# VectorE builds the table of distances before the slopes, in a kernel of banded attention and a two-layer MLP

## Chip, cores and metric

One NeuronCore of a Trainium2 chip. The metric is the device time of one launch in microseconds (us), as the median of several runs. The engines that matter are TensorE (PE in the profile, its weight loads PEld), VectorE (DVE), ScalarE (ACT), GpSimd (POOL) and SyncE (SP). Each has its own in-order queue of instructions; they meet at semaphores. DMAs are issued from the queues of SP, ACT and POOL.

## The reference

Four batches of eight heads, 768 positions, head size 64. A key is kept when it is one of the first 8 positions or lies up to 95 positions behind the query; the score gets a penalty, slope of the head times distance. The attention output goes through two matrix products with `h - tanh(h)` between them.

```python
rel = pos[:, None] - pos[None, :]
is_global = pos[None, :] < 8
is_local = (rel >= 0) & (rel < 96)
keep = is_global | is_local
dist = np.where(is_global & ~is_local, 96.0, np.abs(rel))
slopes = 2.0 ** (-8.0 * (np.arange(H) + 1) / H)
scores = q @ k.T / 8 - slopes[:, None, None] * dist
scores = np.where(keep, scores, -1e9)
a = softmax(scores)
x = (a @ v) as 3072 rows of 512
h = x @ w_in                    # 512 -> 2048
out = (h - tanh(h)) @ w_out     # 2048 -> 512
```

## The kernel before

The 3072 rows are 24 units of 128 query rows (six per batch), the first units of the four batches coming first. For each unit the kernel loads q, k and v, transposes q and k (`T`, copied out of PSUM by `Te`), multiplies them (`S`), takes the exponential on ScalarE (`E`), multiplies by a mask on VectorE (`M`), multiplies by v (`AV`), divides (`R`), transposes (`X`, `Xe`), and runs the MLP in groups of one, two or four units (`m1`, `th`, `g`, `m2`, `ev`, `st`). Since exp(s + b) = exp(s) exp(b), the penalty and the band are one multiplicative mask `mk` that is made once at the start.

That start is what the change touches:

- `rel` (POOL, L237) writes a tile of row minus column, for the unit's own block and the block behind it.
- `slopes` (DVE, L267) is eight instructions, one for each head: a 128x128 diagonal matrix times that head's slope, all from `rel`. The slots of the heads are interleaved: even heads fill slots 0 to 3, odd heads 4 to 7.
- `dist` (DVE, L242, L243, L244) is three instructions, each needing the one before: the distance inside the band, a huge number outside.
- `turn`, `first`, `ident` and `ones.1` follow on VectorE: a permutation matrix for the transposes, the variant of `dist` for a batch's first unit (L247, L248, L251), an identity matrix, and columns of ones in the tiles of v.
- `bm.1` and `bm.0` (PE, L277) multiply `dist` (loaded as weights) by `slopes` (streamed), two matmuls each, one for slots 0 to 3 and one for slots 4 to 7. `em.1` and `em.0` (ACT, L282) take the exponential and leave the mask.
- `zero:7` and its like (PE, L543) are matmuls of a tile of zeros, put there to keep TensorE running; five of them stand ahead of `bm.1`.
- In the same microseconds the first loads go out: `lk.1`, `lk.0` from SP and `lq.1`, `lq.0` from ACT, in float32 (tiles `f`, L296), which `ck`/`cq` then cast (L233 on DVE, L231 on ACT); and from POOL `lk.2`, `lq.2`, `lq.3`, `lk.3` (tiles `kq`, L296), the v tiles (`vb`, L299) and pieces of the MLP's weights (L302), all cast in flight. `T.1`, `T.0` (PE, L319) are the transposes of units 1 and 0, `S.1`, `S.0` (L354) their scores, `AV.1` (L380) the first product with v.

The order on every engine is written out by hand: one string of words, `ORDER`, is walked from left to right, and each word emits its instructions into the queue of its engine. A framework inserts the semaphore waits that the data needs. Buffers are assigned by a second string, so an engine's queue holds its instructions in the order of the words.

Of the kernel before, what the change touches and what calls it, by code (L numbers as in the profile page):

```python
# [14 lines left out]


ORDER = """
lq.1 lk.1 zero rel ones.0 zero:7 slopes lk.2 lq.0 lk.0 zero:7 zero:7 table lq.2 dist zero:7 zero:7 lq.3 turn bm.1
first lk.3 ident bm.0 ones.1 em.1 lv.1 cq.1/d zero:7 ck.1/a lv.0 zero:7 em.0 T.1 in.0 cq.0/a zero:7 ck.0/d lv.2 zero:7
Te.1.0/d Te.1.1/a zero:3 T.0 lv.3 S.1 Te.0.1/d Te.0.0/a zero:6 zero:6 E.1.0 in.1 S.0 T.2 in.3 E.0.0 M.1.0 T.3 in.2  # L20
Te.2.0/d zero:1 Te.2.1/a AV.1 M.0.0 Te.3.0/a lq.4 S.2 Te.3.1/a R.1 AV.0 lk.4 E.2.0 S.3 R.0 E.3.0 in.4 M.2.0 X.0 zero:3
# [569 lines left out]
```

## Time and profile before

| | |
|---|---|
| median of 3 runs | 212.19 us (211.27, 212.39, 212.19) |
| the profiled execution | 212.06 us, of which its span is 210.2 us |
| outside the span | 1.86 us |
| PE busy | 202.4 us (96%) |
| DVE, ACT, POOL busy | 130.0, 121.7, 79.2 us |
| instructions | 4631 |

The span runs from the first to the last instruction that the profiler recorded; times in the timeline are counted from its start. A timeline row gives the start, the time that the merged instructions took together, the engine, the line, the tiles written and read, how many instructions were merged, and in brackets how long the engine had been idle and who released it. Matmul rows of PE overlap, so the distance between two starts says more than the length of one.

### The profile page before, as it was taken

Reading aid. Unit: us, or ns where it says so; the run is one execution under the profiler, and the core shown is the slowest. Engines: PE = TensorE matmul, PEld = TensorE weight load, DVE = VectorE, ACT = ScalarE, POOL = GpSimd, SP = SyncE. Lnnn points to the kernel's source line nnn. Section 1 sums busy time; section 2 is a strip of 40 time slices with the busy share of each in tenths; the row PEclk is TensorE's granted clock in tenths of the full one; section 3 lists DMA queues with packets and bytes.
Section 4 is the critical chain, followed back from the end, with each engine's and each line's share of the span. In section 5 each row is a group of like instructions: output and inputs, shape, how many; then the busy total and the mean of one; then the engine's idle time right before and its main releaser. Section 6 shows DMA issues by size and latency. Waiting matters only on the chain.

```text
span 210.2 us, 4631 instructions
## 1 busy us (share of the span) xinstructions
PE 202.4 (96%) x1851; PEld 122.3 (58%) x1876; DVE 130.0 (62%) x266; ACT 121.7 (58%) x182; POOL 79.2 (38%) x105
## 2 busy tenths in 40 slices
PE   8779999999999999999999999999999999999994
PEld 2459896566867756887655455545544444444443
DVE  6397786353999963878785489757966661711000
ACT  4797783636887464766845687477457552511251
POOL 8976466503995039807509710002000001000350
PEclk9999999999999999999999999999999999999999
DMA  5999999999999989998999999301610001000255
GB/s 162 195 184 199 190 175 203 180 160 181 141 154 187 188 146 186 143 150 148 174 176 160 142 229 171 59 3 48 176 30 0 0 0 50 3 0 0 101 217 182
DMA packets 101348, 27.29 MB, mean 130 GB/s; under 512 B 91856, under 2 KB 99792, under 8 KB 101328
## 3 DMA queue, kind: packets, MB, share of 16 engines
q0 software_dynamic: 73152, 18.88, 86.2%
q1 hardware_dynamic: 27632, 7.61, 21.5%
q10 hardware_dynamic: 544, 0.52, 0.8%
q8 instruction: 14, 0.23, 0.4%
q14 instruction: 6, 0.05, 0.1%
HBM read 27.26 MB, written 6.29 MB: 160 GB/s over the span
## 4 chain that ended last, share of the span: by engine, by line
PE 92%; DMA 3%; DVE 2%; issue 1%; ACT 1%; SPq 0%
PE ps L422 40%; PE ps L447 39%; PE ps L354 5%; PE ps L380 5%; DMA f<-in_k_dram 3%; PE ps L400 1%; DVE pr L365 1%; DVE x L389 1%; ACT pr L361 0%; PE ps L314 0%; SPq L296 0%; PE ps L319 0%; DVE qk L233 0%; ACT qk L231 0%; PE ps L323 0%
## 5 line engine op out<-in xcount | busy, mean ns | idle before, releaser
L422 PE MATMUL ps<-xT,w_in_bf 128*128 128x256 bf16 (+2 forms) x634 | 89.6, 293 | 0.3
L447 PE MATMUL ps<-w_out_bf,g 128*128 128x512 bf16 (+2 forms) x382 | 88.1, 370 | 1.1 <-issue 0.2
L438 DVE TENSOR_TENSOR g<-ps,th 128x512 bf16<-128x512 f32 (+1 forms) x98 | 65.5, 676 | 31.8 <-ACT th L432 30.8
L432 ACT ACTIVATE th<-ps 128x512 f32<-128x512 f32 (+1 forms) x98 | 57.3, 590 | 45.5 <-PE ps L422 40.5
L422 PEld LDWEIGHTS <-w_in_bf 128*128 128x128 bf16 x640 | 56.2, 98 | 27.2
L447 PEld LDWEIGHTS <-g 128*128 128x128 bf16 x400 | 37.1, 98 | 38.7
L456 POOL DMA_DIRECT2D out_dram<-ot x22 | 12.4, 570 | 105.5 <-ACT ot L231 94.9
L361 ACT ACTIVATE pr<-ps 128x1024 bf16<-128x1024 f32 x44 | 42.9, 1027 | 11.4 <-PE ps L354 10.9
L365 DVE TENSOR_TENSOR pr<-pr,mk 128x1024 bf16<-128x1024 bf16 x44 | 29.7, 687 | 11.4 <-ACT pr L361 11.2
L231 ACT COPY ot<-ps 128x512 f32<-128x512 f32 (+2 forms) x20 | 11.3, 564 | 21.0 <-PE ps L447 15.8
L299 POOL DMA_DIRECT2D vb<-in_v_dram x24 | 21.7, 919 | 3.0 <-DMA w_in_bf<-in_moe_w_in_dram 1.7
L299 POOL DMA_DIRECT2D kq<-in_q_dram x19 | 17.3, 916 | 10.0 <-DMA qk<-kq 7.7
L299 POOL DMA_DIRECT2D kq<-in_k_dram x19 | 17.3, 919 | 2.4 <-DMA w_out_bf<-in_moe_w_out_dram 1.6
L389 DVE TENSOR_TENSOR x<-ps,rden 128x512 bf16<-128x512 f32 x24 | 16.6, 691 | 0.8
L380 PEld LDWEIGHTS <-pr 128*128 128x128 bf16 x352 | 13.6, 97 | 4.0 <-DVE pr L365 0.8
L380 PE MATMUL ps<-vb,pr 128*128 128x65 bf16 x352 | 14.6, 193 | 0.1
L354 PEld LDWEIGHTS <-qk 64*128 64x128 bf16 x352 | 9.9, 94 | 6.2 <-issue 4.0
L354 PE MATMUL ps<-qk 64*128 64x128 bf16 x192 | 9.4, 217 | 0.2 <-ACT qk L231 0.2
L354 PE MATMUL ps<-qk,qk 64*128 64x128 bf16 x160 | 7.8, 217 | 0.0
L388 DVE RECIPROCAL rden<-ps 128x8 f32<-128x8 f32 x24 | 4.8, 199 | 4.6 <-PE ps L380 4.4
L233 DVE COPY qk<-qk 128x32 bf16<-128x32 bf16 x16 | 3.3, 221 | 6.5 <-PE ps L354 6.5
L543 PE MATMUL ps<-zero 128*128 128x512 bf16 x14 | 5.3, 483 | 1.0 <-DVE zero L464 1.0
(43 smaller groups left out, 60.3 us busy)
## 6 DMA issues: line engine op xcount, KB each, us to landing
out_dram<-ot POOLq DMA_DIRECT2D x22, 256.0 KB, 2.9
vb<-in_v_dram POOLq DMA_DIRECT2D x24, 128.0 KB, 6.0
kq<-in_k_dram POOLq DMA_DIRECT2D x22, 128.0 KB, 6.2
kq<-in_q_dram POOLq DMA_DIRECT2D x22, 128.0 KB, 6.2
w_out_bf<-in_moe_w_out_dram POOLq DMA_DIRECT2D x4, 512.0 KB, 11.2
w_in_bf<-in_moe_w_in_dram POOLq DMA_DIRECT2D x4, 256.0 KB, 7.6
w_in_bf<-in_moe_w_in_dram POOLq DMA_DIRECT2D x2, 512.0 KB, 10.7
f<-in_q_dram ACTq DMA_DIRECT2D x2, 256.0 KB, 3.9
```

The lines of the kernel that those rows point to most:

```text
L231: nc.scalar.copy(out=out, in_=in_)
L299: eng(e).dma_start(out=dst, in_=rows_of(src, u).rearrange("h p d -> p h d"))
L354: nc.tensor.matmul(bank(("s", u, o), hh)[:, p * P : (p + 1) * P], buf(("qk", back[u] if o else u))[r, 1, p, :], buf(("qk", u))[r, 0, p, :] ...
L361: nc.scalar.activation(d, banks(("s", u, o), 0, 1), AF.Exp, bias=0.0, scale=scale)
L365: nc.vector.tensor_tensor(out=t, in0=t, in1=mk[:, mask_of(u, o)], op=ALU.mult)
L380: nc.tensor.matmul(t[:, h // (H // 2), h % (H // 2), :], buf(("p", u, o))[:, slot(h), :], buf(("v", back[u] if o else u))[:, h, 0 : Dh + 1 ...
L389: nc.vector.tensor_tensor(out=buf(("x", u)).rearrange("q (a h) d -> q a h d", a=2), in0=t[:, :, :, 0:Dh], in1=rden.to_broadcast([P, 2, H / ...
L422: nc.tensor.matmul(t[:, (f - f0) * n : (f - f0 + 1) * n], w_in_bf[j][:, c, fo : fo + P], x[:, c, 0:n], start=(c == 0), stop=(c == CD - 1),)
L432: nc.scalar.activation(h_view(buf(("th", g, f0)), g, m), h_view(bank(("h", g, f0)), g, m), AF.Tanh, bias=0.0, scale=1.0)
L438: nc.vector.tensor_tensor(out=buf(("g", g))[:, f0 : f0 + m, 0:n], in0=h_view(bank(("h", g, f0)), g, m), in1=h_view(buf(("th", g, f0)), g, ...
L447: nc.tensor.matmul(bank(part)[:, 0 : c1 - c0], buf(("g", g))[:, f, t * P : (t + 1) * P], w_out_bf[f // FJ][:, f % FJ, c0:c1], start=(f == ...
L456: eng(e).dma_start(out=out[turn_of[u] * P : (turn_of[u] + 1) * P, c0:c1], in_=buf(("ot", u))[:, c0:c1])
```

## The change

Two words of `ORDER` trade places: `dist` comes where `slopes` stood, and `slopes` where `dist` stood. Between them stand only words of other engines (loads, zero matmuls, and the word `table`, which emits nothing).

```diff
-lq.1 lk.1 zero rel ones.0 zero:7 slopes lk.2 lq.0 lk.0 zero:7 zero:7 table lq.2 dist zero:7 zero:7 lq.3 turn bm.1
+lq.1 lk.1 zero rel ones.0 zero:7 dist lk.2 lq.0 lk.0 zero:7 zero:7 table lq.2 slopes zero:7 zero:7 lq.3 turn bm.1
```

In the built program the instructions of PE, ACT, POOL and SP keep their order. On VectorE the three instructions of `dist` now stand ahead of the eight of `slopes`; `turn` still follows both. The weight load of `bm.1` waits for `dist` as before; before, that wait covered `slopes` too, since they came earlier on the same engine, and now the two matmuls of `bm.1` each have a wait of their own for `slopes`.

## The prediction

> **What bounds the kernel now.** I read the page first: the span, the busy line, the chain that ended last.
>
> ```profile
> span 210.2 us, 4631 instructions
> ...
> PE 92%; DMA 3%; DVE 2%; issue 1%; ACT 1%; SPq 0%
> ```
>
> 92% of the chain is matmuls; the DMA share is a single load. The chain in order of time (start, length, what) says where it lies, and the table of stretches (PE, PEld, DVE, ACT, POOL busy, granted clock, DMA share, GB/s) how the rest runs.
>
> ```profile
> 0.74 0.74 SPq L296
> 1.54 6.23 DMA f<-in_k_dram
> 8.28 0.63 PE ps L319 x8
> ...
> 0.00:8.28 8.28, 5.90 (x23) 2.00 (x23) 3.87 (x32) 4.73 (x6) 7.46 (x14) 1.00 0.82 182
> 8.28:16.00 7.72, 6.49 (x120) 4.52 (x122) 6.50 (x13) 6.83 (x11) 6.51 (x9) 1.00 1.88 178
> 16.00:210.00 194.00, 190.02 (x1713) 115.75 (x1734) 119.66 (x223) 110.13 (x166) 65.22 (x83) 1.00 1.07 126
> ```
>
> So there are two regimes. From 16 us on PE is busy for 190.02 of 194.00 us, and nothing there is touched by the change except by starting earlier or later. Up to 8.28 us the end is set by one transfer: the float32 load of k for unit 0, issued from SP at 1.54, landing at 1.54 + 6.23 = 7.77 us, after which PE's transposes `T.0` start at 8.28. A microsecond won or lost at 8.28 is passed on nearly whole. The mask work that the change reorders lies in that first regime, beside the load. Its timeline:
>
> ```profile
> 0.99 2.31 PE L543 MATMUL ps<-zero 128*128 128x512 bf16 x5 [0.99 <-DVE zero L464]
> 1.21 0.90 DVE L267 TENSOR_SCALAR slopes<-rel 128x128 bf16<-128x128 bf16 x8 [0.23 <-POOL rel L237]
> 1.37 1.03 POOL L296 DMA_DIRECT2D kq<-in_k_dram  x1 [0.19 <-issue]
> ...
> 2.04 0.22 DVE L242 TENSOR_SCALAR far<-rel 128x256 bf16<-128x256 bf16 x1
> ...
> 2.29 0.43 DVE L243 SCALAR_TENSOR_TENSOR far<-rel,far 128x256 bf16<-128x256 bf16 x1
> 2.40 1.45 POOL L296 DMA_DIRECT2D kq<-in_q_dram  x2
> 2.75 0.29 DVE L244 TENSOR_TENSOR dist<-far,rel 128x256 bf16<-128x256 bf16 x1
> 2.96 0.22 DVE L259 TENSOR_SCALAR turn<-rel 128x128 bf16<-128x128 bf16 x1
> 3.09 0.16 PEld L277 LDWEIGHTS <-dist 128*128 128x128 bf16 x2 [0.69 <-DVE dist L244]
> ...
> 3.40 0.43 DVE L254 TENSOR_SCALAR ident<-rel 128x128 bf16<-128x128 bf16 x1
> ...
> 4.20 1.02 ACT L282 ACTIVATE mk<-ps 128x1024 bf16<-128x1024 f32 x1 [0.77 <-PE ps L277]
> ...
> 4.55 1.77 POOL L299 DMA_DIRECT2D vb<-in_v_dram  x2
> ...
> 7.04 0.60 ACT L231 CAST qk<-ps 128x512 bf16<-128x512 f32 x1
> ...
> 7.79 0.43 DVE L233 CAST kq<-f 128x512 bf16<-128x512 f32 x1 [3.01 <-DMA f<-in_k_dram]
> 8.13 1.28 DVE L233 CAST qk<-ps 128x512 bf16<-128x512 f32 x2
> ...
> 8.28 0.62 PE L319 MATMUL ps<-turn,kq 128*128 128x128 bf16 x8 [1.20 <-DVE kq L233]
> 8.87 0.40 PE L354 MATMUL ps<-qk 64*128 64x128 bf16 x8
> ...
> 11.31 0.41 PE L380 MATMUL ps<-vb,pr 128*128 128x65 bf16 x8
> ```
>
> The weight load of `dist` at 3.09 stands 0.69 us idle and names `dist` as its releaser. That looks like a wait worth removing. The next view, single matmuls cut out by narrow windows, says that it isn't.
>
> ```profile
> 2.67 0.63 PE L543 MATMUL ps<-zero 128*128 128x512 bf16 x1
> 3.10 0.63 PE L277 MATMUL ps<-slopes,dist 128*128 128x512 bf16 x1
> ...
> 4.80 0.57 PE L543 MATMUL ps<-zero 128*128 128x512 bf16 x1
> 5.21 0.38 PE L543 MATMUL ps<-zero 128*128 128x512 bf16 x1
> ```
>
> The fifth zero matmul starts at 2.67 and the first of `bm.1` at 3.10, 0.43 us later; from 4.80 to 5.21 it is 0.41. The zeros and the mask products simply follow one another at that pitch, without a gap. The wait of 0.69 us is on PEld, beside matmuls that were running anyway.
>
> **The change, part by part.** It removes and adds no instruction.
>
> *VectorE.* Before, from the first slope to the start of `turn`: 2.96 - 1.21 = 1.75 us. The slopes take 2.04 - 1.21 = 0.83 us from start to start; `dist` needs 0.25 + 0.46 (2.04 to 2.29 to 2.75) and 0.21 until the next instruction may start behind it (2.75 to 2.96). The order of the same steps changes no length by itself: `dist` would run at 1.21, 1.46 and 1.92, done at 1.92 + 0.29 = 2.21; the slopes start at 2.13, the last of eight at 2.13 + 7 x 0.104 = 2.86. One slope takes
>
> ```profile
> L267 DVE TENSOR_SCALAR slopes<-rel x8: 183/186/194, 1.2 to 1.9; 128x128 bf16<-128x128 bf16 x8
> ```
>
> 0.186 us, so it is done at 3.04, and the seventh, the last of the even heads, at 2.94. Before, `dist` was done at 2.75 + 0.29 = 3.04. Both inputs are complete at the same moment either way, only with the other one last. `turn` starts at 2.96 as before, and the copy behind it no longer waits for a fresh `dist`: at most 0.03 us earlier, beside everything.
>
> *TensorE.* The weight load can go early, at about 2.7 instead of 3.09, under the fifth zero. The first matmul of `bm.1` then waits for the seventh slope (2.94), which is sooner than its turn at 3.10 behind the zeros; so 3.10 stays. Gain: 0. Were the zeros gone, the gain would still end at 2.94, 0.16 us earlier. Queued behind that wait on PE are the second product, `bm.0`, two zeros and `T.1`. And even a later mask costs nothing at first: ACT's chain starts with the mask at 4.20 and runs without a pause to the copy that ends at 7.04 + 0.60 = 7.64, and `S.1` at 8.87 also waits for VectorE's copy, the first of the two from 8.13 that take 1.28 together, so up to 8.77: 1.1 us of slack. Cover: the load landing at 7.77. Without that load, up to 0.2 us would show.
>
> *POOL.* No word moves on POOL, but its first DMA issue (1.37, `lk.2`) takes 1.03 us where the two behind it take 0.72 each (1.45 for both). It ran beside the eight slopes and `far`, and ended at 2.40, 0.14 us after `far` (2.04 + 0.22 = 2.26). Later `ident`, of the slopes' shape, takes 0.43 us where a slope takes 0.186, and ends at 3.83, where POOL's third issue ends (2.40 + 1.45 = 3.85). I read both as the two engines holding each other up. In the new order the first issue lies beside `far`, 0.22 us of that kind, and then the two instructions with two inputs; if these don't hold POOL, it ends at 1.37 + 0.72 = 2.09, 0.31 us earlier. The slopes then meet the second issue, which loses about what the first gained. So of the POOL queue only `lk.2` moves: 0 if its 1.03 us is its own, -0.31 if the slopes made it.
>
> The Trainium skill ("SBUF — State Buffer", section "SBUF: two separate sides") says that VectorE in a two-port mode and GpSimd exclude each other for a whole instruction, and that GpSimd can then write no DMA descriptors. The two rows above agree in kind. By it alone the first issue, once behind the slopes' train, would wait to the train's end; that is the second rival.
>
> *What an earlier `lk.2` costs.* The DMA queues, windows of 0.5 us (packets, MB, share of 16 engines), first from 4.3 to 4.8 and then from 4.8 to 5.3, and last from 5 to 6 us:
>
> ```profile
> q10 hardware_dynamic: 173, 0.17, 97.6%
> q1 hardware_dynamic: 17, 0.01, 7.9%
> ...
> q0 software_dynamic: 93, 0.05, 74.5%
> q10 hardware_dynamic: 51, 0.04, 23.9%
> q1 hardware_dynamic: 21, 0.02, 15.5%
> ...
> q1 hardware_dynamic: 121, 0.12, 44.3%
> ```
>
> q0 is POOL's queue, q10 ACT's, q1 SP's, on which the decisive k is last. As soon as q0 begins, at 4.8, the two float32 queues fall from 0.18 to 0.06 MB in half a microsecond. Beginning 0.31 us sooner takes (0.18 - 0.06) x 0.31 / 0.5 = 0.074 MB from them, which q1 wins back at 0.12 MB per us: up to 0.6 us on the landing at 7.77. The lower end is 0. I take 0.2, a third, because a part of what is lost belongs to q10, which has slack, and because the 1.03 us may be the first issue's own.
>
> *Sum.* 212.06 (profiled execution) + 0 (VectorE) + 0 (PE) + 0.2 (load of k) = 212.3. The profiled execution lies 0.13 us under the median of 212.19, well inside the scatter of 1.1 us of the three runs, so I leave the sum as it is. With the ends 0 and 0.6 and that scatter, this case spans 211.3 to 213.1. 0.5% of the time is 1.06 us, about what a measurement of this kernel can tell from no change.
>
> **The rivals.**
>
> *First, slower: TensorE reaches its full rate later.* The pitch of 128x512 matmuls was 0.43 us up to 4.80, and the last zeros show it falling (0.57 us long at 4.80, 0.38 at 5.21): the full rate came at about 5.2 us, after 4.2 us of unbroken matmuls since 0.99. My margin for the slopes is thin: 3.10 - 2.94 = 0.16 us. If one of them is held as `ident` was (0.43 - 0.186 = 0.24 us), the row of matmuls gets a gap of 0.1 us or more, and if 4.2 unbroken microseconds are wanted, the count starts again. The next such stretch begins at 8.28, behind the 1.20 us pause: full rate at 12.5, and the path from 8.28 to 12.5 at half the rate costs up to half of it, 2.1 us: 214.2. It decides as soon as the matmul at 3.10 starts visibly later. Against it: a gap of 0.1 in 4 us is little, and the slopes were not held up before, though POOL's first issue ran beside them. The Trainium skill ("TensorE: Matmul & The Clock Gate", section "What you observe" and the text after it) has a free-running window of about 3.4 us of activity instead of an unbroken count. By that a short gap would hardly matter; this trace, with one change of rate, cannot tell.
>
> *Second, faster: POOL's first issue is caught by the slopes.* If its 1.03 us is its own, it is still running at 2.13 when the slopes start; held to the end of `turn` (2.96 + 0.22) plus the 0.14 seen above, it ends at 3.32 instead of 2.40. q0 then starts 0.92 us later, and the float32 loads land sooner. The limit is ACT, whose last cast and copy end at 7.64: `T.0` and `S.1` could come up to 8.87 - 7.7 = 1.1 us earlier, 211.0. The first `AV.1` (11.31) needs v, issued at 4.55 and landing 6.0 later, at 10.55:
>
> ```profile
> vb<-in_v_dram POOLq DMA_DIRECT2D x1, 128.0 KB, 6.0
> ```
>
> If that landing stays, 0.76 us is the most that gets through, 211.3; if it moves with the issue, nothing. For it: the hold-ups are in the rows. Against it: the slopes did not stop the first issue for their full length before either.
>
> *Third, the change does nothing at all,* all hidden behind the load: 212.1. I count it in the forecast's case.
>
> **How the numbers follow.** Forecast's case, nothing but small shifts of the load: 0.66, of which 0.02 each lie beyond 0.5% by scatter. TensorE's rate: 0.16, of which 0.14 are slower by over 0.5%. POOL caught: 0.18, half beyond 0.5%, since its price runs from 0 to -1.1 us. Faster 0.02 + 0.09 = 0.11, slower 0.02 + 0.14 = 0.16, same 0.73. The range takes in the forecast's case, the second rival to its end of 211.0 and the first with a price a little under the full one: 211.0 to 213.9.
>
> **What would show it.** In the profile after: `dist` done near 2.2 and the last slope near 3.04 on DVE; PEld's load of `dist` under the fifth zero, and PE's first mask product still at 3.10 (later means the first rival, to be seen again in the length of `T.0` at 8.28, 0.62 us now). POOL's first issue near 0.72 us (forecast) or over 1.1 (second rival). The cast of k at 7.79 some 0.2 later, or clearly earlier. I am wrong if the time moves by over 1.06 us while these starts stay, or if the stretch behind 16 us gives or takes time of its own.

## The result, and the profile after

The changed kernel takes 211.88 us in the median of 22 runs (211.17 to 215.60), the kernel before 212.18 us in the median of 22 (211.27 to 212.91). The ratio of the means is 0.9975, with a 95% interval of 0.9963 to 0.9987: half a microsecond faster by the means, 0.30 us by the medians. In three later comparisons of the same two kernels (below) the ratio was 0.9992, 0.9976 and 0.9996, each with an interval that reaches over 1, so the size of the gain is not settled. Mean and median hide the form of it, and the form is the finding. The times fall into bunches:

| times of the 22 runs, us | before | changed |
|---|---|---|
| 211.17 to 211.56 | 2 | 8 |
| 211.77 to 212.03 | 0 | 8 |
| 212.05 to 212.91 | 20 | 3 |
| 214.52 to 215.60 | 0 | 3 |

The last row is slower executions, which the ratio leaves out and the median of 211.88 doesn't (with them the means would be 212.14 and 212.19): in the one that was profiled (214.52 us) k of unit 0 landed at 9.22 us, some two microseconds late, and the kernel before has such times in later comparisons (up to 214.49). So the fastest runs are hardly faster than the fastest before (211.17 against 211.27); more runs are near 211.3, and the bunch behind that lies lower.

The profile after that I read (`after_timed` below) is of an execution of 211.89 us, from the second bunch. The page and the chain of waits up to 9 us:

```profile
span 210.1 us, 4631 instructions
...
PE 92%; DMA 3%; DVE 2%; issue 1%; ACT 1%; SPq 0%
```

```profile
1.54 5.83 DMA f<-in_k_dram
7.37 0.02 issue
7.39 0.69 DVE kq L233
8.08 0.05 issue
8.13 0.64 PE ps L319 x8
```

The same chain as before: k of unit 0, its cast, `T.0`. The load lands at 7.37 instead of 7.77, but the cast that follows takes 0.69 us, and `T.0` starts at 8.13 instead of 8.28. The timeline around it:

```profile
1.22 0.23 DVE L242 TENSOR_SCALAR far<-rel 128x256 bf16<-128x256 bf16 x1 [0.24 <-POOL rel L237]
1.38 0.86 POOL L296 DMA_DIRECT2D kq<-in_k_dram  x1 [0.19 <-issue]
...
1.94 0.29 DVE L244 TENSOR_TENSOR dist<-far,rel 128x256 bf16<-128x256 bf16 x1
...
2.15 0.98 DVE L267 TENSOR_SCALAR slopes<-rel 128x128 bf16<-128x128 bf16 x8
2.24 1.45 POOL L296 DMA_DIRECT2D kq<-in_q_dram  x2
2.68 0.15 PEld L277 LDWEIGHTS <-dist 128*128 128x128 bf16 x1 [0.27 <-issue]
...
3.10 1.91 PE L277 MATMUL ps<-slopes,dist 128*128 128x512 bf16 x4
...
4.20 1.02 ACT L282 ACTIVATE mk<-ps 128x1024 bf16<-128x1024 f32 x1 [0.78 <-PE ps L277]
...
7.03 0.62 ACT L231 CAST kq<-f 128x512 bf16<-128x512 f32 x1 [0.38 <-DMA f<-in_q_dram]
7.39 0.68 DVE L233 CAST kq<-f 128x512 bf16<-128x512 f32 x1 [2.77 <-DMA f<-in_k_dram]
...
8.13 0.62 PE L319 MATMUL ps<-turn,kq 128*128 128x128 bf16 x8 [1.04 <-DVE kq L233]
```

Everything on PE and ACT up to 5 us is where it was: the mask products at 3.10, the first mask at 4.20. What moved is POOL's queue (the first issue 0.86 us instead of 1.03, the second at 2.24 instead of 2.40) and ACT's cast of q (7.03, waiting for its load, instead of 6.54). Behind 16 us nothing gives or takes time. Stretches of the same lengths as before, moved by the 0.15 us (PE, PEld, DVE, ACT, POOL busy, clock, DMA share, GB/s):

```profile
8.13:15.85 7.72, 6.49 (x120) 4.52 (x122) 6.50 (x13) 6.84 (x12) 6.55 (x10) 1.00 1.88 179
15.85:209.85 194.00, 190.02 (x1713) 115.72 (x1734) 120.28 (x223) 110.16 (x166) 65.24 (x83) 1.00 1.06 126
```

6.49 and 190.02 us of PE, as before. In fourteen of the twenty profiles of this study the time is the start of `T.0` plus a constant, for example 7.44 and 211.23, 7.48 and 211.26, 7.52 and 211.31, 7.84 and 211.70, 8.13 and 211.89, 8.24 and 212.02, 8.28 and 212.06; the difference is 203.76 to 203.86 in each. The other six are the three in which the loads came late (`T.0` at 8.99 to 9.73, difference 204.8) and the three of set 3, in which POOL's queue waits (205.6 to 206.6). For the two kernels the question is what sets that start.

### The profile page after: what moved, and what is told of

It is laid out like the page before. It is cut to its first block, busy times and chain, and to the rows that moved or that the text cites. A ratio compares the mean times of both kernels' runs of the same rounds, so it can differ in the third digit from the quotient of the medians.

```text
span 212.7 us, 4631 instructions
## 1 busy us (share of the span) xinstructions
PE 204.1 (96%) x1851; PEld 123.4 (58%) x1876; DVE 130.9 (62%) x266; ACT 122.1 (57%) x182; POOL 79.3 (37%) x105
## 4 chain that ended last, share of the span: by engine, by line
PE 92%; DMA 4%; DVE 1%; issue 1%; SPq 0%; ACT 0%
PE ps L422 39%; PE ps L447 39%; PE ps L354 5%; PE ps L380 5%; DMA f<-in_k_dram 4%; PE ps L400 1%; PE ps L323 1%; PE ps L543 1%; DVE x L389 1%; PE ps L319 0%; PE ps L314 0%; SPq L296 0%; DVE qk L233 0%; DVE pr L365 0%; DVE kq L233 0%
## 5 line engine op out<-in xcount | busy, mean ns | idle before, releaser
L354 PE MATMUL ps<-qk 64*128 64x128 bf16 x192 | 9.9, 225 | 0.0
L233 DVE COPY qk<-qk 128x32 bf16<-128x32 bf16 x16 | 4.0, 273 | 6.5 <-PE ps L354 6.5
L543 PE MATMUL ps<-zero 128*128 128x512 bf16 x14 | 6.0, 540 | 1.0 <-DVE vb L273 1.0
```

The lines of the kernel that those rows point to most:

```text
L354: nc.tensor.matmul(bank(("s", u, o), hh)[:, p * P : (p + 1) * P], buf(("qk", back[u] if o else u))[r, 1, p, :], buf(("qk", u))[r, 0, p, :] ...
```

## The experiments

Each kernel ran beside the kernel before on the same chip, twelve runs where times are listed. "Early" below is a time up to 211.7 us. There were five such sets behind the result: the kernel before was early in 10 of 23, 13 of 35, 1 of 35, 12 of 29 and 10 of 29 of its runs. Each set ran on one chip, another one each time. So shares are compared only inside one set.

**Set 1: the two kernels again, and a small memset on POOL.**

> The changed kernel again, for a profile of an undisturbed execution and its times beside the kernel before. Theory L (load): POOL's first issue is held for less time by VectorE, POOL's queue q0 starts its transfer earlier, shares the DMA engines with ACT's load of q instead of with SP's load of k, and k of unit 0 lands earlier than the 7.77 us of before: about 7.1, T.0 at 7.7 instead of 8.28, time 0.5 us under before. Theory W (weights): the weight load of dist that moves from 3.09 to 2.67 brings the mask and with it T.0 forward: ACT's mask before 4.15 us, k's landing unchanged at 7.8. Theory N (nothing): all starts within 0.1 us of before and times equal within 0.1%.

Measured: 211.51 us, ratio 0.9992 (0.9972 to 1.0013), 7 of 12 early, four others at 211.87 to 211.92. The profile is the one above. Theory W is out: the weight load did move to 2.68 and the first mask stayed at 4.20. N is out by the starts, which moved by more than 0.1 us. L is half right: k landed at 7.37, not at 7.1, and something beside the landing made the cast long.

> The kernel before, a second profile of it, to see how far the landing of k of unit 0 (7.77 us) and the start of q0's transfers (4.79 us) vary between executions of one and the same kernel. Theory L: landing 7.5 to 8.0, q0 at 4.7 to 4.9. Theories W and N say nothing of it.

Measured: 211.31 us. The kernel before can land k early as well:

```profile
7.03 0.43 DVE L233 CAST kq<-f 128x512 bf16<-128x512 f32 x1 [2.25 <-DMA f<-in_k_dram]
...
7.52 0.62 PE L319 MATMUL ps<-turn,kq 128*128 128x128 bf16 x8
```

The expectation of 7.5 to 8.0 was wrong: between two executions of one kernel the landing differs by 0.76 us (7.01 and 7.77), more than the 0.40 us between the profiles before and after. The one profile on which the prediction rests was of a late landing.

A second profile of the changed kernel (`after_look`), in which theory L expected k at 6.9 to 7.3, was of an execution of 214.35 us with late loads: k landed at 9.04. It tells nothing about the theories.

```diff
-... ones.0 zero:7 dist lk.2 ...
+... ones.0 zero:7 dist pad lk.2 ...
+op(("pad",), POOL, lambda e: nc.gpsimd.memset(padt, 0.0))      # padt: 128x128 bf16
```

> The changed kernel with one POOL memset of a 128x128 tile that nobody reads put in front of POOL's first DMA issue, so that this issue ends about 0.1 to 0.2 us later, where it ended before the change. Theory L: q0 starts later again, k of unit 0 lands near 7.8 and the time goes back to that of before (ratio 0.999 to 1.001). Theory W: nothing on PE or VectorE is touched, the time stays at the 0.9975 of the changed kernel. Theory N: 1.000 both.

Measured: 211.35 us, ratio 0.9974 (0.9944 to 1.0004), 9 of 12 early; two of the others at 212.03 and 212.06. The memset was to delay the first issue, and didn't. It (0.195 us) fitted into the gap in front of the first issue, which stayed at 1.39 and short (0.86). The second issue took 0.88 us instead of 0.74, so that the queue from the third issue on stood at 3.12, 3.83, 4.54, where it stood before the change. That splits the two things: first issue as changed, later queue as before.

**Set 2: what holds the cast.** The casts of 0.43 and 0.68 us differ in what POOL is doing. In the profile after, POOL's issue of v for unit 2 runs from 6.90:

```profile
6.90 0.91 POOL L299 DMA_DIRECT2D vb<-in_v_dram  x1
```

It ends at 7.81, and the cast, started at 7.39, at 8.07, 0.26 us later. From this came theory G (the cast is held by the issue), and a POOL wait to test it, in both kernels:

```diff
-... ck.0/d lv.2 ...
+... ck.0/d gate lv.2 ...
+op(("gate",), POOL, lambda e: nc.gpsimd.tensor_copy(out=padt, in_=buf(("kq", 0))[:, 1, 0:8]))
```

> The kernel before, with POOL made to wait, ahead of its issue of v of unit 2, for VectorE's cast of k of unit 0 (a POOL copy of 8 columns of the cast's result, which nobody reads further, stands there). Theory G (held cast): the float32 cast on VectorE is held while POOL is issuing a DMA and ends 0.23 us after that issue; in the kernel before, the issue of v of unit 2 ends at 7.95, so every landing of k between about 7.2 and 7.9 gives T.0 at 8.25 and 212.05 us, and a landing by 7.0 gives 7.45 and 211.25. With POOL waiting, the cast takes 0.43 us whenever k lands: the bunch at 212.05 to 212.25 goes, the times below 212.0 grow to over half, and the median falls to 211.3 to 211.7. Theory D (DMA alone): the two bunches are landing times of k; the wait changes nothing, the bunch at 212.05 to 212.25 stays with its share.

> The changed kernel with the same wait on POOL. Theory G: no difference left to the kernel before with that wait (medians within 0.15 us, 211.3 to 211.7), and the bunch of the changed kernel at 211.86 to 211.92 is gone. Theory D: the bunch at 211.9 stays, 0.15 under that of the kernel before.

Measured: 211.89 us, ratio 0.9986 (0.9960 to 1.0011), 5 of 12 early, and 211.50 us, ratio 0.9979 (0.9951 to 1.0006), 9 of 12 early. The strongest sign for G is the profile of the second. k landed almost when it did in the profile after (7.34 and 7.37), POOL was issuing nothing, and the cast was short:

```profile
7.36 0.43 DVE L233 CAST kq<-f 128x512 bf16<-128x512 f32 x1 [2.74 <-DMA f<-in_k_dram]
```

`T.0` started at 7.84, in an execution of 211.70 us. The times say less. No run of the two lies at 212.05 to 212.12 or at 211.86 to 211.92, but of the range 212.05 to 212.25 that G wanted empty two of 12 runs are left (212.14 and 212.17), against 11 of 35 of the kernel before: in so few runs the bunch cannot be called gone. And the medians are not equal, the kernel before did not come down to 211.7: some landings are late in themselves, as D has it.

```diff
-... em.1 lv.1 ...
+... em.1 pad lv.1 ...
+op(("pad",), POOL, lambda e: nc.gpsimd.memset(padt, 0.0))      # padt: 128x512 bf16
```

> The kernel before, with a POOL memset of about 0.48 us that nobody reads, after its fourth DMA issue, so that v of units 1, 0 and 2 and the first weights are issued about 0.45 us later. Theory G: the ends of the issues move along, that of the first weights from 7.05 to 7.5 and that of v of unit 2 from 7.95 to 8.4. A k that lands by 7.0 now meets the issue of the weights: T.0 at 7.8, 211.6 instead of 211.25; a late one meets v of unit 2: T.0 at 8.7, 212.5 instead of 212.05. Theory D: the bunches stay at 211.25 and 212.05.

Measured: 212.28 us, ratio 1.0016 (0.9990 to 1.0042), 2 of 12 early, a bunch of four at 212.68 to 212.72, none at 212.05 to 212.15. The memset moved the queue by 0.64 us, not 0.45:

```profile
4.55 0.69 POOL L467 MEMSET padt<- 128x512 bf16 x1
5.19 1.77 POOL L299 DMA_DIRECT2D vb<-in_v_dram  x2
...
7.69 0.92 POOL L299 DMA_DIRECT2D vb<-in_v_dram  x1
```

212.05 + 0.64 = 212.69: the bunch follows POOL's queue to a few hundredths. Theory D, by which bunches are landing times, is out for it. Two things remain: the profiled execution (211.98 us) is not one of the bunch, and the two early runs (211.31 and 211.43) are not at the 211.6 that G gave for them.

```diff
-... zero:7 slopes lk.2 ...
+... zero:7 slopes pad lk.2 ...
+op(("pad",), POOL, lambda e: nc.gpsimd.memset(padt, 0.0))      # padt: 128x1024 bf16
```

> The kernel before, with a POOL memset of about 0.86 us that nobody reads in front of its first DMA issue, so that POOL's whole queue starts 0.6 to 0.9 us later. The prediction's step (an earlier POOL transfer takes from the load of k): the other way round, k lands up to 1.4 us earlier, its middle engine at 6.0 instead of 6.6 to 6.7. Theory Q (POOL's transfers at that time share with ACT's load of q): the middle engine of k stays at 6.5 to 6.8, that of q stays at 5.3 or falls. Theory G: the cast meets another issue, so T.0 moves with the issue's end.

Measured: 211.45 us, ratio 0.9991 (0.9962 to 1.0019), six of ten runs at 211.43 to 211.45. In the profiled execution (211.82 us) k landed at 6.38, and its cast met an issue:

```profile
2.04 0.86 POOL L296 DMA_DIRECT2D kq<-in_k_dram  x1
...
3.80 1.89 PE L277 MATMUL ps<-slopes,dist 128*128 128x512 bf16 x4 [0.49 <-DVE dist L244]
...
6.41 0.75 DVE L233 CAST kq<-f 128x512 bf16<-128x512 f32 x1 [1.42 <-DMA f<-in_k_dram]
...
8.06 0.61 PE L319 MATMUL ps<-turn,kq 128*128 128x128 bf16 x8
```

A POOL queue that starts 0.67 us later does relieve the load of k, and theory Q, by which k stays where it is, is out. The gain was lost because the memset held VectorE's slopes: the mask products came at 3.80 instead of 3.10, and TensorE's queue ran from there to `T.0` almost without a pause. The cast was held too (it ended at 7.16), but `T.0` waited longer for the rest of its queue.

**Set 3: POOL later, by waits instead of memsets.** All three keep VectorE's changed order. `after_wait` has a POOL copy of 8 columns that VectorE sets between L242 and L243; `after_late` a POOL copy of 8 columns of `dist`; `quiet_pool` the same and `gate`, with `lv.0 in.0 lv.2` behind it.

> The changed kernel, with POOL's first DMA issue made to wait about a quarter of a microsecond (a POOL copy of 8 columns that VectorE sets between the first two instructions of dist), so that it ends at 2.45 to 2.5, about 0.05 to 0.1 us later than before the change, and POOL's queue behind it too. VectorE's order stays the changed one. Theory P (POOL is all of it): the gain is gone, q0's transfers start at 4.3 to 4.8 again, k lands late as often as in the kernel before, the held cast's bunch stands at 212.05 to 212.15, ratio 0.999 to 1.001. Theory O (VectorE's or TensorE's own order): the gain stays, 0.997 to 0.9985.

Measured: 212.63 us, ratio 1.0015 (0.9993 to 1.0037), none of 12 early. The copy itself took long (0.41 us, against 0.19 in `after_late`), and the first issue came at 1.90 and ended at 2.75, 0.35 us later than before the change instead of 0.05 to 0.1. k then landed at 6.27 and `T.0` started at 7.05, among the earliest of the study, and the time was nevertheless 212.66. The start is not the whole story here:

```profile
115.99 1.04 PE L422 MATMUL ps<-xT,w_in_bf 128*128 128x512 bf16 x4 [0.75 <-DMA xT<-x]
```

`T.0` had gained 1.23 us on the kernel before. TensorE lost 0.14 of it by 20 us, 0.30 near 65 us and 0.92 near 116 us (0.75 of that is this wait for a transposing transfer), so the whole gain and 0.13 us more. The other half microsecond lies outside the span: 2.1 to 2.4 us in all twelve of these runs, where about seven in eight of the other runs of the study have 1.8 to 1.9. Why is open. As a test of P it failed, since it moved more than it should.

> The changed kernel, with POOL's whole queue made to wait for dist (a POOL copy of 8 columns of it): POOL's first issue at about 2.4 instead of 1.38. If a later POOL transfer relieves the load of k, as the kernel with the memset showed (landing 6.38), k lands at 6.0 to 6.4, and without the memset the mask stays at 4.2; the cast of k then meets another issue and is held to its end, T.0 at 7.4 to 7.7, 211.2 to 211.5, and the bunch above 212 is gone. If the landing is set by a late DMA engine whatever POOL does, the times spread as in the kernel before.

Measured: 211.80 us, ratio 0.9979 (0.9952 to 1.0005), 5 of 12 early, the fastest 211.13. In the profile k landed at 6.45, its cast took 0.43 us instead of being held, and `T.0` started at 6.96; that execution took 213.27 us all the same, and four runs lie above 212.5: the expected end of the tail did not come.

> The same as the one with the whole queue waiting for dist, and besides POOL waits for the cast of k before it issues v of unit 0, the first weights and v of unit 2 (those three stand behind the cast). Theory G: no issue is under way when k lands, the cast takes 0.43, T.0 is set by ACT's cast of q (ended 7.16): T.0 at 7.2 to 7.4, 211.0 to 211.15, under both kernels, with a spread of under 0.3 us. Rival: v and the weights, now up to 1 us later, come late for the first product with v or the first MLP matmuls, and the time is 211.4 or more.

Measured: 213.12 us, ratio 1.0007 (0.9980 to 1.0035), none early. k's cast took 0.43 us and `T.0` started at 6.87, as G has it, but the rival was right about the time, the v tiles were late (waits of PE, us in total, times, longest):

```profile
PE ps L380 <- DMA vb<-in_v_dram: 1.3, 2, 0.9
```

> The changed kernel once more, on the chip of these comparisons, for its share of times under 211.7 us. Theory P: 50 to 60% of its times lie there, against 35 to 40% of the kernel before, the bunch of its held cast stands at 211.86 to 211.92, ratio 0.997 to 0.9995. Theory N (no difference on this chip): the same share as the kernel before and no bunch of its own.

Measured: 211.76 us, ratio 0.9976 (0.9949 to 1.0004), 6 of 12 early, three at 211.87 and 211.88. In that set the kernel before was early in 1 of 35 runs.

**Sets 4 and 5: the first issue and the later queue apart.** `six_first` splits `slopes` into six and two with `dist` between them; `pad_again` and `trio_pad` repeat the small memset; `after_nudge` and `trio_nudge` have it with 400 columns, so that the first issue ends at 2.37, about where it ended before (2.40); `trio_after` is the changed kernel.

> Only the last part of the change: six slopes, then dist, then the other two slopes. dist is done at 2.85 instead of 3.04 (before) or 2.23 (after), so TensorE's and VectorE's order is nearly that of before, but the run of slopes that POOL's first issue meets ends with the first instruction of dist near 2.05 instead of 2.25. Theory P (only POOL's first issue matters): that issue takes 0.85 to 0.9 us as in the changed kernel, q0's transfers start at 3.9 to 4.2, k lands by 7.0 in about half of the runs, the held bunch is at 211.86 to 211.92, ratio 0.997 to 0.999. Theory O (the order on VectorE or TensorE): as before, 0.9995 to 1.0005, bunch at 212.05.

Measured: 211.94 us, ratio 1.0003 (0.9973 to 1.0033), 5 of 12 early against 12 of 29. The first issue was 0.86 us, as expected of the run of slopes that ended sooner, and POOL's queue behind it stood as in the changed kernel. P therefore wanted a bunch at 211.86 to 211.92, and no run lies there: four of the others are at 211.93 to 212.00, between the two bunches. That is a miss for P; the ratio's interval takes in what P and O expected of it, so it does not tell them apart.

> The kernel with the small POOL memset again: its first issue is short and early as in the changed kernel, while from the third issue on POOL's queue stands where it stood before the change. Theory P, in two parts: the share of runs under 211.7 is that of the changed kernel (half or more, set by the first transfer), and the held bunch stands at 212.03 to 212.07 (set by the queue's later issues), not at 211.87. If instead the later queue is what sets the share, it falls to that of the kernel before.

Measured: 211.96 us, ratio 0.9998 (0.9966 to 1.0029), 5 of 12 early, two of the others at 212.06. The place of the bunch is as expected, the share isn't above that of the kernel before.

> The changed kernel with a POOL memset of 400 columns in front of the first issue, which moves that issue by 0.1 to 0.2 us, to where it ended before the change. The memset also holds VectorE's first instruction of dist by up to 0.3 us, so that the mask may come 0.2 us later (hidden by the load of k). Theory P: q0's transfers start at 4.2 to 4.8, the share of runs under 211.7 falls to that of the kernel before, the bunch is at 212.0 to 212.15. Theory O: the share stays at half.

Measured: 212.03 us, ratio 0.9990 (0.9970 to 1.0011), 3 of 12 early, seven at 212.03 to 212.05. The profile shows why so many have one time:

```profile
7.04 0.91 POOL L299 DMA_DIRECT2D vb<-in_v_dram  x1
...
7.38 0.83 DVE L233 CAST kq<-f 128x512 bf16<-128x512 f32 x1 [2.61 <-DMA f<-in_k_dram]
8.26 0.51 PE L319 MATMUL ps<-turn,kq 128*128 128x128 bf16 x6 [1.10 <-DVE kq L233]
```

k landed when it did in the profile after (7.38 and 7.39). The issue ends 0.14 us later (7.95 instead of 7.81), the cast also (8.21 instead of 8.07, again 0.26 behind the issue), `T.0` too (8.26 instead of 8.13), and so does the bunch (212.04 instead of 211.88).

> The changed kernel, one of three on one chip. Theory P (first transfer sets the share): its share of times under 211.7 us is above that of the kernel before, and the held bunch is at 211.86 to 211.92. Theory C (the share belongs to the chip, the change moves the bunch alone): the share is that of the kernel before within chance.

> Short first POOL issue, later queue as before. Theory P: the share of the changed kernel, bunch at 212.03 to 212.07. Theory C: the share of the kernel before, bunch at 212.03 to 212.07.

> VectorE's changed order with the first POOL issue ending where it ended before. Theory P: the share of the kernel before, below that of the other two; bunch at 212.03 to 212.05. Theory C: all shares equal within chance, bunch at 212.03 to 212.05.

Measured, with 10 of 29 early for the kernel before: 3 of 12, 12 of 12 and 1 of 12; three runs at 211.86 to 211.89 in the first and four at 212.01 to 212.03 in the last; medians 211.89, 211.30 and 212.08 us, ratios 0.9996 (0.9968 to 1.0023), 0.9967 (0.9950 to 0.9984) and 1.0002 (0.9975 to 1.0028). Theory C does not fit 12 of 12 beside 1 of 12. P does not fit 3 beside 12. With the small memset k's cast got away just ahead of the issue:

```profile
6.99 0.43 DVE L233 CAST kq<-f 128x512 bf16<-128x512 f32 x1 [2.22 <-DMA f<-in_k_dram]
...
7.04 0.91 POOL L299 DMA_DIRECT2D vb<-in_v_dram  x1
```

The share of early runs inside the sets: the two memset kernels ran together in sets 4 and 5 and differ in the first issue, while their queue from the third issue on is the same to 0.02 us (with 400 columns the first mask also comes 0.08 us later). The small memset (short first issue) was early in 17 of 24 runs, the one with 400 columns (first issue as before) in 4 of 24, the kernel before in 22 of 58. k landed at 6.93 to 7.02 in the three profiles of the first and at 7.34 and 7.35 in the two of the second.

The changed kernel, with the short first issue and the earlier queue, was early in 7 of 12, 6 of 12 and 3 of 12 runs of sets 1, 3 and 5, beside 10 of 23, 1 of 35 and 10 of 29 of the kernel before (and in 8 of 22 beside 2 of 22 in the result): clearly more often in one of the three sets. This fits a pair of causes, a short first issue that lets k land sooner and a later issue of v that leaves a k of 7.0 us time to be cast; both are argued from these counts and rows, not shown, and `six_first` (short first issue, k at 6.95 in its profile, no larger share) does not help them.

The version with the small memset beats both kernels in the last set. In the others its ratio to the kernel before was 0.9974 and 0.9998 with intervals that reach over 1, so a gain is shown in one set of three.

## Why the prediction was wrong

The sign was wrong: 212.3 forecast, a shift of +0.2 us, where -0.5 us was measured. It lay inside the range, and "within 0.5%" was the likeliest class and came true, but by the width of the range and not by the mechanism.

*What bounds the kernel:* right. `T.0`'s start passes to the end one for one, in the fourteen profiles named above.

*VectorE and TensorE:* right in the result. `dist` was done at 2.23 (2.21 forecast), the weight load went to 2.68, the products stayed at 3.10, ACT's mask at 4.20. The slopes took longer than summed, since the fifth, sixth and seventh (0.41, 0.34 and 0.27 us) stood until POOL's second issue ended at 2.98 (ns, least, median, longest of the eight):

```profile
L267 DVE TENSOR_SCALAR slopes<-rel x8: 176/185/408, 2.2 to 3.0; 128x128 bf16<-128x128 bf16 x8
```

The margin of 0.16 us took it: the last of the even heads' slopes, the first to be needed, was done at 3.04 instead of 2.94, and the first rival (a gap in front of the mask products) did not happen. In `after_nudge` the products did start 0.13 us later (3.23), and `T.0` still took 0.62 us and the rest of the time its constant: a gap of that size had no such price there.

*POOL: mis-sized, and one step failed.* The first issue fell from 1.03 to 0.86 us, not to 0.72: 0.17 us won of 0.31 forecast. "The slopes then meet the second issue, which loses about what the first gained" failed: the second issue took 0.74 as before, VectorE was the one held, and the whole POOL queue came 0.17 us earlier, to the issue of v at 6.90. The second rival (POOL caught by the slopes) did not happen: the first issue ended at 2.24, 0.09 us after the slopes had begun, and was not held by them. The Trainium skill's rule that I weighed ("SBUF — State Buffer", "SBUF: two separate sides": whichever starts first has the port, the other blocks) agrees with who was held here only in part. The slopes that stood had met an issue already under way, but the three before them, started at 2.25, 2.36 and 2.46 under the same issue (from 2.24), took their bare 0.185 us. And with the small memset, where all starts differ by 0.01 us, it was the issue that gave way (0.88 us).

*The load of k: the step that failed, and with it the sign.* The +0.2 us were to come from q0 taking bandwidth from SP's load of k. q0 did start earlier, by more than the issue did (its first packet at 3.93 instead of 4.79), and did take bandwidth, but from the other float32 load, that of q. Queues of the profile after, from 4.3 to 4.8 us, from 4.8 to 5.3 and from 5 to 6; last ACT's queue from 5 to 6 in the profile before:

```profile
q0 software_dynamic: 102, 0.05, 75.7%
q10 hardware_dynamic: 68, 0.07, 50.0%
q1 hardware_dynamic: 3, 0.00, 1.4%
...
q10 hardware_dynamic: 89, 0.09, 61.9%
q0 software_dynamic: 76, 0.04, 56.1%
q1 hardware_dynamic: 9, 0.01, 5.7%
...
q10 hardware_dynamic: 158, 0.15, 49.3%
q1 hardware_dynamic: 132, 0.14, 38.9%
...
q10 hardware_dynamic: 16, 0.01, 3.7%
```

From 4.3 to 4.8 us q10 moved 0.07 MB instead of 0.17, while q1 had moved only 0.01 there before and had nothing to lose. From 5 to 6 us q10 still moved 0.15 MB where before it was done (0.01), and q1 moved 0.14 against 0.12. The loss went to q, which has slack: it landed at 7.01 instead of 5.70 (ACT's cast at 7.03 instead of 6.54). The other profiles agree, leaving out the three with late loads: with the short first issue (seven profiles) q landed at 6.42 to 7.01 and k at 6.93 to 7.37; in four of the kernel before and its variants with the same first issue q landed at 5.68 to 6.15 and k at 6.95 to 7.77. (In the two with 400 columns q landed at 5.66 and 6.91, so the first issue is not all that moves it.) By 6 us SP's queue had moved 0.36 to 0.40 MB in the seven and 0.39 to 0.43 in the four, so a small loss of k is not excluded, but its landings don't show it. I had named q's slack for a part of the loss; it took what can be seen of it. The rows of the prediction pointed there: the fall from 0.18 to 0.06 MB at 4.8 us was that of q10, which had then moved 0.48 of its 0.52 MB.

The mechanism itself is not void. Where POOL's queue came 0.35 us or more later than before the change (`before_late` and set 3), k landed at 6.27 to 6.45 in all four profiles. SP's queue from 4.8 to 5.3 us in `before_late`, where it had moved 0.02 MB in the profile before:

```profile
q1 hardware_dynamic: 146, 0.15, 85.6%
```

*What was left out.* The hold of VectorE by a POOL issue was in the prediction, for `ident`, but I didn't carry it to the cast of k, which meets POOL's queue in the same way and lies on the path. That is where the queue's 0.17 us come out: the bunch at 212.05 moved to 211.88. The profile before does not show it at that cast, which started at 7.79, 0.17 us before the issue ended, and took its bare 0.43 us. But its other cast of a float32 load was held, to 0.22 us after POOL's fourth issue:

```profile
3.84 0.71 POOL L296 DMA_DIRECT2D kq<-in_k_dram  x1
...
4.29 0.48 DVE L233 CAST kq<-f 128x512 bf16<-128x512 f32 x1 [0.19 <-DMA f<-in_q_dram]
```

And I took the landing of 7.77 for the kernel's, where it was one execution's.

What is shown: the cast is held by the issue that it meets (the rows above, and the short cast behind `gate`), and the place of the bunch follows the end of the issue of v (212.69, 212.04, 211.88 for ends at 8.61, 7.95, 7.81); `six_first` is the exception. By an estimate from the two lists of times (mean of the runs above 211.7 us: 212.27 before, 211.99 changed without the slowest three; early 2 of 22 and 8 of 19), the lower place of the late runs makes about 0.2 of the 0.5 us, and the larger share of early runs about 0.3. What is open is that larger part: why the landing of k scatters between 6.9 and 7.8 at all, and why the share of late landings differs so much from set to set. No profile of the kernel before itself has a held cast of k; its bunch is explained from the memset kernels, whose issue of v stands at the same time.

## What to carry to other kernels

A wait in a profile is worth what is late next: here the weight load stood 0.69 us idle beside matmuls that ran, and removing that wait moved nothing on TensorE. A reordering on one engine can act through the engine that it shares something with; look for operations that take longer than their like, and for the same pair of engines further down the path. Where the end of a stage is a DMA landing, one profile is one draw: look at a second one, and at the list of times for bunches, before arguing in tenths of a microsecond.

## What the runs showed that I had not expected

A float32 cast on VectorE that meets a DMA issue of POOL in its middle ends about a quarter of a microsecond after the issue (8.07 and 8.21 after 7.81 and 7.95), which makes times of a kernel fall into bunches of a few hundredths of a microsecond. In 18 of the 20 profiles, 21 casts of 128x512 started 0.28 to 0.50 us into an issue, and all ended 0.22 to 0.26 us after it. It works both ways and only in a part of the issue: with `six_first` the cast started 0.08 us into an issue, took its bare 0.43 us, and the issue took 0.99 us instead of 0.91. Three other casts that started 0.01 to 0.06 us into an issue also took 0.43.

A later POOL queue is no free gain: in `after_wait`, half a microsecond more than in the changed kernel brought k in at 6.27 us, and 0.92 us came back near 116 us, 0.75 of it in a wait for a transfer, where no row near the start pointed to it.

The time and the span are not the same thing: in about one in eight of the runs 2.1 us or more lie outside the span instead of 1.8 to 1.9, so such a run comes out up to 0.6 us longer than its work.
